# Block-sparse attention and a Gelu feed-forward on one core: sampled copies on VectorE alone, value loads tied to the feed-forward, values two rounds behind

## The chip, the core and the metric

One core of a Trainium2 chip runs the whole program. The metric is the device time of one execution in microseconds (us). The engines are named as the profile names them: PE (TensorE), DVE (VectorE), ACT (ScalarE), POOL (GpSimd), SP (SyncE). TensorE has two clock levels, 1.2 and 2.4 GHz; a granted clock of 1.00 is the upper one.

## The reference, cut to what matters

```python
# q, k, v: (4 batches, 8 heads, 768 rows, 64); blocks of 32 rows, 24 blocks; sampled_blocks: (24, 3)
scores = (q @ k.T) / 8
mask = |blk_i - blk_j| <= 1, or blk_i in (0, 23), or blk_j in (0, 23), or blk_j in sampled_blocks[blk_i]
attn = softmax(where(mask, scores, -1e9))
x    = (attn @ v), heads side by side          # (3072, 512)
out  = gelu_exact(x @ w_in) @ w_out            # 512 -> 2048 -> 512
```

## The kernel before

The work is cut into eight units: four batches times two halves of 12 blocks (384 rows). A unit's attention is followed by its first feed-forward product (FFN1: eight steps of eight 128x384 matmuls and one Gelu each, g holds the result), and its second one (FFN2: three output tiles of 16 matmuls) is cut into 48 pieces that fill the next unit's attention. The order on every engine is written out by hand; each engine runs its queue in order.

Attention goes by rounds. A first half has four dense rounds (blocks 0 and 23 see everything) and six sparse rounds of two query blocks; a second half has six sparse rounds. A round is: scores on PE (L218, 64x32 tiles of the array), a maximum on DVE (L252, L255), exponentials on ACT (L264), a 32x32 transpose on DVE (L281). Two rounds at a time then go through values on PE (L289, 128 small matmuls and as many weight loads), divided on DVE (L331), and outputs (L345: PE transposes, an ACT copy to xT). The scores buffers are two, the values buffer one. A sparse query block scores against three neighbours, blocks 0 and 23, and three sampled blocks: three products per head for each block.

The sampled blocks' keys and values are first copied into gb (L196): one copy for each of the 66 (block, sample) pairs of a batch, its source address in a register. DVE does 15 of them and POOL 51, into one gb for each half. For batch 0 keys and values are copied apart, since values come later. The registers are read once, at the start (L154).

The first unit has no feed-forward to hide behind (first_attention, L424): all its rounds run first, then DVE gathers its 15 value blocks, then come its values. When the next unit is a new batch, FFN1 is interleaved with prep (L168: PE transposes of k and q, copied into place by DVE for k and ACT for q), and the gather stands on DVE between the k part and the next unit's first maximum (L485 to L489).

All loads are issued by POOL, in its own order, behind its copies: for the next batch k, q and eight value loads (L474 to L480) are issued as the first half's FFN1 begins. The value loads have rows of 64 elements for each head.

Of the kernel before, what the change touches and what calls it, by code (L numbers as in the profile page):

```python
# [19 lines left out]
def kernel(  # L20
# [11 lines left out]
    P = 128  # L32
# [12 lines left out]
    BW = KC + 2 * V2  # L45
    PI = 8
# [4 lines left out]
    UB = NB // 2  # L51
    US = UB - 1
    NE = S // BL // 2
# [15 lines left out]
    gbs = [const.tile([P, US, NR, BW], BF16, name=f"gb{i}") for i in range(2)]  # L69
# [8 lines left out]
    g = const.tile([P, KOUT, UT], BF16, name="g")  # L78

    HALVES = (slice(0, 4), slice(4, 8))  # L80

# [24 lines left out]

    raw = const.tile([1, NB, NR, 2], I32, name="raw")
# [13 lines left out]

    def value_frame(i, engine):
        kv = kvs[i]
        engine.memset(kv[:, :, KC:BW], 0.0)
        for hh in range(4):
            c0 = KC + VW * (hh % 2) + D
            engine.memset(kv[32 * hh:32 * hh + 32, 0:NB, c0:c0 + V2 + 1:V2], 1.0)

# [5 lines left out]
    rf = const.tile([1, NB, NR], F32, name="rf")  # L134
    vf = const.tile([1, NB, NR], F32, name="vf")

    def value_list():
        inv = const.tile([1, NB, NR], F32, name="inv")
        tmp = const.tile([1, NB, NR], F32, name="tmp")
        nc.vector.tensor_copy(rf, raw[:, :, :, 0])  # L140
        nc.vector.tensor_tensor(tmp, rf, jrow, op=ALU.subtract)
        nc.vector.tensor_tensor(tmp, tmp, tmp, op=ALU.mult)
        nc.vector.tensor_scalar(inv, tmp, 1.0, None, op0=ALU.is_le)
        for c in (0.0, float(NB - 1)):
            nc.vector.tensor_scalar(tmp, rf, c, None, op0=ALU.is_equal)
            nc.vector.tensor_tensor(inv, inv, tmp, op=ALU.max)
        for a, c in ((1, 0), (2, 0), (2, 1)):
            nc.vector.tensor_tensor(tmp[:, :, 0], rf[:, :, a], rf[:, :, c], op=ALU.is_equal)
            nc.vector.tensor_tensor(inv[:, :, a], inv[:, :, a], tmp[:, :, 0], op=ALU.max)
        nc.vector.tensor_scalar(tmp, rf, -1.0, float(NB), op0=ALU.mult, op1=ALU.add)  # L150
        nc.vector.tensor_tensor(tmp, tmp, inv, op=ALU.mult)
        nc.vector.tensor_tensor(vf, rf, tmp, op=ALU.add)

    def block_numbers(js, engine):  # L154
        m = len(js)
        idx = const.tile([1, m, NR], I32, name=f"idx_{engine.name}_{js[0]}")
        nc.vector.tensor_copy(idx, vf[:, js[0]:js[0] + m, :])
        flat = idx.rearrange("o j r -> o (j r)")
        vals = []
        for c0 in range(0, m * NR, 22):  # L160
            c1 = min(c0 + 22, m * NR)
# [4 lines left out]
        return {(js[i // NR], i % NR): x for i, x in enumerate(vals)}  # L166

    def prep(b, which, pr, on_act):  # L168
        src = kn if which == "k" else qn
        pt = psT.tile([P, PI, PP], BF16, name="pt", tag="T")  # L170
        for i in range(PI):
            for h2 in range(2):
# [3 lines left out]
                                    identity[0:PP, 0:PP])  # L176
        if which == "k":
# [14 lines left out]
    def spare_key(b, engine):  # L192
        kT = keys(b)
        engine.tensor_copy(kT[:, NB, :], kT[:, 0, :])  # L194

    def gather(b, js, vals, engine, src=None, c0=0, c1=BW):  # L196
        src = kvs[b % 2][:, :, c0:c1] if src is None else src
        for j in js:
            gb = gbs[(j - 1) // US]
            for r in range(NR):  # L200
                engine.tensor_copy(gb[:, (j - 1) % US, r:r + 1, c0:c1],  # L201
                                   src[:, bass.ds(vals[j, r], 1), :])

    def gather_keys(js, vals, engine):
        gather(0, js, vals, engine, k0, 0, KC)

    def gather_values(js, vals, engine):
        gather(0, js, vals, engine, None, KC, BW)

    def rounds_of(hf):  # L210
        j0 = 1 + US * hf
        js = list(range(j0, j0 + US))
        dense = [("d", x, G) for x in (0, 1) for G in (0, 1)] if hf == 0 else []
        return dense + [("s", tuple(js[i:i + 2])) for i in range(0, US, 2)]
# [3 lines left out]
    def scores(b, rnd):  # L218
        qT, kT = qTs[b % 2], keys(b)
# [8 lines left out]
        if rnd[0] == "s":  # L228
            A4 = A.rearrange("p (g j c) -> p g j c", g=2, j=2)
            for i, j in enumerate(rnd[1]):  # L230
                gb = gbs[(j - 1) // US]
# [57 lines left out]
    def values(b, hf, grp):  # L289
        kv = kvs[b % 2]  # L290
# [13 lines left out]
        else:  # L304
            slots = [(rnd, i, j) for rnd in grp for i, j in enumerate(rnd[1])]
            for G in range(2):
                c0 = KC + V2 * G
                for c in range(8):
                    for s, (rnd, i, j) in enumerate(slots):
# [5 lines left out]
                        elif c < 5:  # L315
                            blk = (0, NB - 1)[c - 3]
                            blk = NB if abs(blk - j) <= 1 else blk
                            src = kv[:, blk, c0:c0 + V2]
                        else:
                            src = gbs[hf][:, (j - 1) % US, c - 5, c0:c0 + V2]  # L320
# [24 lines left out]
    def outputs(hf, grp):  # L345
# [7 lines left out]
        if grp[0][0] == "s":  # L353
            t0 = (grp[0][1][0] - UB * hf) * BL
            nc.scalar.copy(xTs[hf][:, :, t0:t0 + 32 * n], T[:, :, 0:32 * n])  # L355
        else:
            Tv = T[:, 0:2, :].rearrange("p h (g x q) -> p g h x q", g=2, x=2)
            for x, t0 in ((0, 0), (1, UT - BL)):
                nc.scalar.copy(
                    xTs[x][:, :, t0:t0 + BL].rearrange("p (g h) q -> p g h q", g=2), Tv[:, :, :, x, :])  # L360

    def ffn1_step(hf, m):
        hp = psA.tile([P, 2, 512], F32, name="hp", tag="A")
        for i in range(2):
            for ki in range(KIN):
                nc.tensor.matmul(hp[:, i, 0:UT], lhsT=w_in_sb[:, ki, (m + i) * P:(m + i + 1) * P],  # L366
                                 rhs=xTs[hf][:, ki, :], start=(ki == 0), stop=(ki == KIN - 1))
        nc.scalar.activation(g[:, m:m + 2, :], hp[:, :, 0:UT], AF.Gelu)  # L368

    def ffn2_pieces(b, hf):  # L370
        for t in range(UT // P):
# [8 lines left out]
            row = b * S + hf * UT + t * P  # L380
# [3 lines left out]
    def grouped(rounds, hf):  # L384

        ends = {}
        r0 = 0
        if hf == 0:
            ends[3] = tuple(rounds[0:4])
            r0 = 4  # L390
        for i in range(r0, len(rounds), 2):
            ends[min(i + 1, len(rounds) - 1)] = tuple(rounds[i:i + 2])
        return ends

    def attention(b, hf, filler):
        rounds = rounds_of(hf)
        n = len(rounds)
        ends = grouped(rounds, hf)
        late = 12
        per = -(-(KOUT * (UT // P) - late) // (n + 1))  # L400

        def fill(m):
            for _ in range(m):
                next(filler, None)
        for it in range(-1, n + 2):
            if it + 1 < n:
                scores(b, rounds[it + 1])
# [6 lines left out]
            fill(per // 2 if it <= n - 1 else late // 4)  # L414
            if it - 2 in ends:
                outputs(hf, ends[it - 2])
            if it - 1 in ends:
                values(b, hf, ends[it - 1])
                divided(ends[it - 1])
            fill(per - per // 2 if it <= n - 1 else late // 4)  # L420
        for _ in filler:
            pass

    def first_attention(fetch):  # L424

        rounds = rounds_of(0)
        n = len(rounds)
        for it in range(-1, n + 1):
            if it + 1 < n:
                scores(0, rounds[it + 1])  # L430
            if 0 <= it - 1 < n:
                turned(rounds[it - 1])
            if it + 1 < n:
                maxima(rounds[it + 1])
            if 0 <= it < n:
                exponentials(rounds[it])
        fetch()
        groups = list(grouped(rounds, 0).values())
        for i, grp in enumerate(groups):
            values(0, 0, grp)  # L440
            divided(grp)
            if i:
                outputs(0, groups[i - 1])
        outputs(0, groups[-1])

    units = [(b, hf) for b in range(B) for hf in range(2)]
    DVE, POOL = mybir.EngineType.DVE, mybir.EngineType.Pool
    J0, J1 = list(range(1, 1 + US)), list(range(1 + US, 1 + 2 * US))
    value_list()
    v_dve = block_numbers(J0[:5], DVE)  # L450
    v_pool0 = block_numbers(J0[5:], POOL)
    v_pool1 = block_numbers(J1, POOL)
    for pr in range(NPR):
        prep(0, "k", pr, False)
    for pr in range(NPR):
        prep(0, "q", pr, True)
    spare_key(0, nc.vector)
    gather_keys(J0[5:], v_pool0, nc.gpsimd)
    gather_keys(J0[:5], v_dve, nc.vector)
# [4 lines left out]
    gather_values(J0[5:], v_pool0, nc.gpsimd)  # L464
    gather_keys(J1, v_pool1, nc.gpsimd)
    gather_values(J1, v_pool1, nc.gpsimd)
    value_frame(1, nc.gpsimd)
    first_attention(lambda: gather_values(J0[:5], v_dve, nc.vector))

    for u, (b, hf) in enumerate(units):  # L470
        nxt = units[u + 1] if u + 1 < len(units) else None
        fresh = nxt is not None and nxt[1] == 0
        if hf == 0:
            if b + 1 < B:  # L474
# [51 lines left out]
```

## Time and profile before

| | us |
|---|---|
| median of 3 runs (range) | 410.44 (406.65 to 411.94) |
| profiled execution | 407.97 |
| its span | 405.8 |
| busy: PE, DVE, ACT, POOL | 280.7, 196.6, 202.8, 146.5 |

Busy shares say little here: no engine is busy more than 69% of the span, and each stage has its own limit. The profile is read by the chain of work that ended last, in order of time, and then by the stretch in which the chain waits.

### The profile page before, as it was taken

How to read it: one execution, taken by the hardware profiler on the slowest of the kernel's cores; microseconds unless marked ns; L12 is line 12 of the kernel's file. 1: busy time of each engine (PE TensorE's matmuls, PEld its weight loads, DVE VectorE, ACT ScalarE, POOL GpSimd, SP SyncE). 2: the span in 40 equal slices, each digit the busy share in tenths (PEclk: the TensorE clock that was granted, in tenths of full speed). 3: DMA queues.
4: the chain of work that ended last, by engine and by line, in shares of the span. 5: the costliest groups of instructions: out<-in, count | busy, mean ns of one | idle time of the engine just before them, and what ended most of it. 6: DMA issues, size and time to landing. Idle time of an engine off the chain costs nothing.

```text
span 405.8 us, 15457 instructions
## 1 busy us (share of the span) xinstructions
PE 280.7 (69%) x6889; PEld 161.2 (40%) x6952; DVE 196.6 (48%) x332; ACT 202.8 (50%) x344; POOL 146.5 (36%) x321
## 2 busy tenths in 40 slices
PE   0353304298789886697889764497789776977895
PEld 0222203144345353354444432254455343634542
DVE  6568993103636885106549771106538773065100
ACT  1057300057645775358456861258446764684531
POOL 8299997000002997100009992000007950000000
PEclk9999999999999999799999999599899999999999
DMA  8989709900010009920000049900000000000001
GB/s 125 105 100 206 118 0 162 75 0 2 31 53 4 1 31 153 117 20 29 31 27 2 28 69 162 61 0 31 29 28 2 29 29 31 0 29 29 29 26 52
DMA packets 39203, 20.90 MB, mean 52 GB/s; under 512 B 25825, under 2 KB 36066, under 8 KB 39138
## 3 DMA queue, kind: packets, MB, share of 16 engines
q0 software_dynamic: 35680, 13.63, 53.3%
q1 hardware_dynamic: 3458, 6.29, 4.2%
q8 instruction: 54, 0.88, 0.9%
q14 instruction: 11, 0.09, 0.1%
HBM read 27.26 MB, written 6.29 MB: 83 GB/s over the span
## 4 chain that ended last, share of the span: by engine, by line
PE 52%; DVE 18%; issue 15%; ACT 12%; DVEq 1%; ACTq 0%
PE hp L366 19%; PE op L374 13%; PE av L323 9%; ACT pp L264 7%; DVE gb L201 6%; PE sc L226 5%; PE pt L174 3%; DVE xh L340 3%; DVE nm L252 3%; ACT os L379 2%; ACT L264 2%; PE tx L350 2%; DVE nm L255 1%; PE av L299 1%; ACT xT L355 1%
## 5 line engine op out<-in xcount | busy, mean ns | idle before, releaser
L201 POOL COPY gb<-kv 128x388 bf16 (+1 forms) x204 | 88.6, 487 | 156.7 <-PE hp L366 101.5
L374 PE MATMUL op<-w_out_sb,g 128*128 128x512 bf16 x321 | 88.0, 384 | 19.6 <-ACT os L379 10.9
L264 ACT ACTIVATE pp<-sc,nm 128x256 bf16<-128x256 f32 (+1 forms) x192 | 92.6, 597 | 13.4 <-DVE nm L252 9.0
L366 PE MATMUL hp<-xT,w_in_sb 128*128 128x384 bf16 x512 | 95.7, 345 | 4.5 <-ACT xT L355 4.5
L252 DVE TENSOR_REDUCE nm<-sc 128x4 f32<-128x1024 f32 (+1 forms) x48 | 53.8, 1121 | 66.0 <-PE sc L226 65.3
L368 ACT ACTIVATE g<-hp 128x768 bf16<-128x768 f32 x64 | 51.9, 811 | 42.5 <-PE hp L366 42.5
L366 PEld LDWEIGHTS <-w_in_sb 128*128 128x128 bf16 x512 | 50.9, 103 | 41.3 <-issue 13.6
L323 PEld LDWEIGHTS <-pT 64*32 64x32 bf16 x2816 | 29.0, 98 | 65.6 <-issue 42.9
L323 PE MATMUL av<-kv,pT 64*32 64x130 bf16 x1760 | 29.0, 239 | 37.1 <-DVE xh L340 18.8
L374 PEld LDWEIGHTS <-g 128*128 128x128 bf16 x384 | 31.3, 98 | 38.3 <-issue 11.4
L226 PEld LDWEIGHTS <-qT 64*32 64x32 bf16 x2240 | 22.2, 93 | 50.4 <-issue 39.0
L336 DVE TENSOR_SCALAR den<-av 128x8 f32<-128x8 f32 (+2 forms) x28 | 4.8, 170 | 73.0 <-PE av L323 70.6
L201 DVE COPY gb<-kv 128x388 bf16 (+1 forms) x60 | 39.1, 838 | 1.1 <-DVE kv L194 1.0
L355 ACT COPY xT<-tx 128x512 bf16<-128x512 bf16 (+1 forms) x24 | 13.2, 552 | 49.0 <-PE tx L350 49.0
L379 ACT COPY os<-op 128x512 f32<-128x512 f32 x24 | 14.1, 588 | 42.5 <-PE op L374 27.5
L281 DVE STREAM_TRANSPOSE pT<-pp 128x512 f32<-128x512 f32 (+1 forms) x48 | 30.8, 653 | 5.7 <-ACT pp L264 5.5
L226 PE MATMUL sc<-kv,qT 64*32 64x96 bf16 (+3 forms) x1152 | 23.1, 211 | 10.5 <-ACT pp L264 9.7
L92 POOL DMA_DIRECT2D kv<-in_v_dram x32 | 22.7, 716 | 20.4 <-DMA qn<-in_q_dram 13.4
L323 PE MATMUL av<-gb,pT 64*32 64x130 bf16 x1056 | 21.5, 241 | 9.4 <-issue 9.4
L226 PE MATMUL sc<-gb,qT 64*32 64x96 bf16 x704 | 22.8, 214 | 3.6 <-issue 3.6
L188 ACT ACTIVATE qT<-pt 128x768 bf16<-128x768 bf16 x16 | 12.9, 806 | 20.3 <-PE pt L174 20.3
L183 DVE COPY kv<-pt 128x768 bf16<-128x768 bf16 x12 | 11.5, 958 | 17.0 <-PE pt L174 17.0
(50 smaller groups left out, 198.1 us busy)
## 6 DMA issues: line engine op xcount, KB each, us to landing
out_dram<-os SPq DMA_DIRECT2D x24, 256.0 KB, 2.1
kn<-in_k_dram POOLq DMA_DIRECT2D x8, 384.0 KB, 6.1
qn<-in_q_dram POOLq DMA_DIRECT2D x8, 384.0 KB, 9.1
kv<-in_v_dram POOLq DMA_DIRECT2D x32, 96.0 KB, 12.1
w_in_sb<-in_moe_w_in_dram POOLq DMA_DIRECT2D x4, 512.0 KB, 8.3
w_out_sb<-in_moe_w_out_dram POOLq DMA_DIRECT2D x2, 1024.0 KB, 18.1
raw<-in_sampled_blocks_dram SPq DMA_DIRECT2D x1, 0.6 KB
```

Of the source, the lines that this page charges most:

```text
L92: nc.gpsimd.dma_start(out=kvs[b % 2][32 * hh:32 * hh + 32, 0:NB, c0:c0 + D], in_=v[b, h].rearrange("(n p) d -> p n d", p=BL))
L201: engine.tensor_copy(gb[:, (j - 1) % US, r:r + 1, c0:c1], src[:, bass.ds(vals[j, r], 1), :])
L226: nc.tensor.matmul(o, lhsT=qT[rows, pr, BL * j:BL * j + BL], rhs=rhs[rows, :, BL * pr:BL * pr + BL], start=True, stop=True)
L252: nc.vector.tensor_reduce(out=nm[:, 0:2 * n].rearrange("p (g j) -> p g j", g=2), in_=A4[:, :, 0:n, :], op=ALU.max, axis=AX.X, negate=True)
L264: nc.scalar.activation(dst.rearrange("p (c k e) -> p c e k", e=2, k=BL), src.rearrange("p (c e k) -> p c e k", e=2, k=BL), AF.Exp, bias=bias)
L281: nc.vector.transpose(pt[:, 0:w].bitcast(F32), pp[:, 0:w].bitcast(F32))
L323: nc.tensor.matmul(av[32 * s:32 * s + 32, h, V2 * G:V2 * G + V2], lhsT=pv[rows, c // 2, :, c % 2], rhs=src[rows], start=(c == 0), stop=(c ...
L355: nc.scalar.copy(xTs[hf][:, :, t0:t0 + 32 * n], T[:, :, 0:32 * n])
L366: nc.tensor.matmul(hp[:, i, 0:UT], lhsT=w_in_sb[:, ki, (m + i) * P:(m + i + 1) * P], rhs=xTs[hf][:, ki, :], start=(ki == 0), stop=(ki == K ...
L368: nc.scalar.activation(g[:, m:m + 2, :], hp[:, :, 0:UT], AF.Gelu)
L374: nc.tensor.matmul(op, lhsT=g[:, m, t * P:(t + 1) * P], rhs=w_out_sb[:, m, :], start=(m == 0), stop=(m == KOUT - 1))
L379: nc.scalar.copy(os, op)
```

## The change

- POOL copies nothing any more. DVE does all sampled copies (33 for each unit), into one gb for both halves. The registers of the first half's blocks are kept; those of the second half are read anew by DVE in each batch, in two parts.
- A slot of gb has five blocks: keys of block 0, three sampled, keys of block 23 (two broadcast copies, gather_ends). A sparse block then has two score products per head, not three.
- In the first unit the eight transposed k and q tiles each have a PSUM space of their own, all placed by ACT.
- Value loads of batch b+1 or b+2 go four at a time behind the first Gelu of an FFN1 (hold_loads: a POOL copy of one element of g); k and q loads go behind its last Gelu. In the head, four value loads of batch 1 are issued after the weights.
- In a round the order on PE becomes scores, values (two rounds behind), outputs (three behind), FFN2 pieces. Groups of rounds follow the tiles of 128 rows.

```diff
-    gbs = [const.tile([P, US, NR, BW], BF16, name=f"gb{i}") for i in range(2)]
+    gb = const.tile([P, US * GW + BW - KC], BF16, name="gb")
+    def hold_loads(m):
+        nc.gpsimd.tensor_copy(mark, g[0:1, m, 0:1])
...
+    def gather_ends(b, n):
+        ends = gb[:, 0:GW * n].rearrange("p (j c) -> p j c", c=GW)
+        for c0, blk in ((0, 0), (4 * BW, NB - 1)):
+            nc.vector.tensor_copy(ends[:, :, c0:c0 + KC],
+                                  keys(b)[:, blk:blk + 1, :].to_broadcast([P, n, KC]))
+    def gather(b, js, *spans):
+        for k0_, k1 in ((0, len(js)),) if js[0] in known else ((0, 6), (6, len(js))):
+            part = js[k0_:k1]
+            at = known if js[0] in known else block_numbers(part, DVE)
+            for i, j in enumerate(part, k0_):
+                for r in range(NR):
+                    for c0, c1 in spans:
+                        src = keys(b) if c1 == KC else kvs[b % 2][:, :, c0:c1]
+                        nc.vector.tensor_copy(slot(i)[:, 1 + r:2 + r, c0:c1],
+                                              src[:, bass.ds(at[j][r], 1), :])
...
                 for c0, c1, rhs in ((0, 96, kT[:, j - 1:j + 2, :]),
-                                    (96, 160, kT[:, 0:NB:NB - 1, :]),
-                                    (160, 256, gb[:, (j - 1) % US, :, :])):
+                                    (96, 256, slot(unit.js.index(j)))):
...  (attention)
+        tail = (4, 9)
+        share = max(0.0, pieces - sum(tail)) / (n + 3)
+        for it in range(-1, n):
+            if it + 1 < n:
+                scores(unit, rounds[it + 1])
+            if it - 2 in ends:
+                values(unit, ends[it - 2])
+            if it >= 1:
+                turned(rounds[it - 1])
+            if it + 1 < n:
+                maxima(rounds[it + 1])
+            if it - 2 in ends:
+                divided(ends[it - 2])
+            if it >= 0:
+                exponentials(rounds[it])
+            if it - 3 in ends:
+                outputs(unit, ends[it - 3])
+            fill(share * (2 if it < 1 else 1))
...  (head)
-    gather_keys(J0[5:], v_pool0, nc.gpsimd)
-    gather_keys(J0[:5], v_dve, nc.vector)
+    for i, (which, pr) in enumerate([(w, pr) for w in "kq" for pr in range(NPR)]):
+        turn_heads(which, pr, spaces[i])
+        place_heads(0, which, pr, spaces[i], True)
+    spare_key(0)
+    gather(0, units[0].js, (0, KC))
+    gather_ends(0, len(units[0].js))
...
+    value_frame(1, nc.gpsimd, 5)
+    for h in range(4):
+        load_v(1, h)
...  (loop over units)
+        if nxt is not None and not fresh:
+            if b == 0:
+                gather(0, nxt.js, (0, KC), (KC, BW))
+            else:
+                gather(b, nxt.js, (0, BW))
+            gather_ends(b, len(nxt.js))
         for s in range(KOUT // 2):
+            ffn1_step(n, 2 * s)
+            if s == 0:
+                if not fresh and b + 1 < B:
+                    hold_loads(0)
+                    for h in range(4, H):
+                        load_v(b + 1, h)
+                if fresh and b + 2 < B:
+                    hold_loads(0)
+                    for h in range(4):
+                        load_v(b + 2, h)
+            if s == 7 and not fresh and b + 1 < B:
+                hold_loads(14)
                 for hs in HALVES:
                     load_kq(kn, k, b + 1, hs)
```

## Rows read from the trace of the kernel before

**Rows 1.** The page: the span, and the queue that brings instructions.

```profile
span 405.8 us, 15457 instructions
...
q8 instruction: 54, 0.88, 0.9%
```

**Rows 2.** The chain that ended last, in order of time: start us, length us, what.

```profile
67.20 2.34 issue
...
73.32 6.53 issue
...
82.66 13.12 PE hp L366 x64
...
136.37 0.87 DVE nm L255
...
168.19 13.10 PE hp L366 x64
...
221.41 0.87 DVE nm L255
...
251.02 6.12 issue
...
260.41 13.00 PE hp L366 x64
...
298.12 1.46 PE hp L366 x8
...
314.43 0.87 DVE nm L255
...
329.10 1.52 issue
...
379.11 10.56 PE hp L366 x64
```

**Rows 3.** Timeline of the head: start us, us, engine, line, work [idle before, releaser].

```profile
12.72 0.71 POOL L92 DMA_DIRECT2D kv<-in_v_dram  x1 [1.24 <-DMA qn<-in_q_dram]
...
18.58 0.85 PE L174 MATMUL pt<-identity,qn 96*64 96x96 bf16 x16 [1.05 <-DVE qT L183]
...
19.47 0.81 ACT L188 ACTIVATE qT<-pt 128x768 bf16<-128x768 bf16 x1 [17.44 <-PE pt L174]
...
25.49 1.91 DVE L255 TENSOR_REDUCE nm<-sc 128x1 f32<-128x768 f32 x2 [3.44 <-PE sc L226]
...
42.19 11.52 POOL L201 COPY gb<-kv 128x260 bf16 x33
...
44.32 17.56 DVE L201 COPY gb<-kv 128x260 bf16 x15
...
62.63 0.74 PE L323 MATMUL av<-kv,pT 64*32 64x130 bf16 x40 [17.13 <-DVE xh L340]
```

**Rows 4.** DVE's copies beside POOL's and alone (timelines); the register reads (by line).

```profile
129.30 7.08 DVE L201 COPY gb<-kv 128x388 bf16 x15 [0.39 <-DVE kv L194]
...
60.81 0.70 DVE L201 COPY gb<-kv 128x260 bf16 x4
...
18.80 0.45 DVE L201 COPY gb<-qT 128x128 bf16 x3
...
L162 DVEq TENSOR_LOAD <-idx_DVE x1: 1778/1778/1778, 9.9 to 9.9; - x1
```

**Rows 5.** Stretches: length, busy PE, PEld, DVE, ACT, POOL; granted clock, DMA share, GB/s.

```profile
238.00:249.00 11.00, 6.23 (x216) 3.15 (x218) 5.14 (x10) 5.29 (x12) 7.23 (x11) 0.84 1.05 171
249.00:259.00 10.00, 2.97 (x105) 1.85 (x104) 1.52 (x5) 0.92 (x2) 0.73 (x2) 0.81 3.72 79
...
343.94:354.50 10.56, 10.56 (x77) 6.23 (x83) 0.00 (x0) 6.93 (x8) 0.00 (x0) 1.00 0.04 15
```

**Rows 6.** Timeline of one sparse round in a second half.

```profile
275.24 0.45 PEld L226 LDWEIGHTS <-qT 64*32 64x32 bf16 x48 [0.42 <-issue]
...
275.88 1.23 DVE L252 TENSOR_REDUCE nm<-sc 128x4 f32<-128x1024 f32 x1 [0.68 <-PE sc L226]
```

More of the change, by code (lines that the diff above doesn't have):

```diff
@@ L204, in gather_keys, with prep @@
[L204 to L214, printed above, removed]
+    def prep(b, which, pr, on_act):
+        pt = psT.tile([P, PI, PP], BF16, name="pt", tag="T")
+        turn_heads(which, pr, pt)
+        place_heads(b, which, pr, pt, on_act)
@@ new lines, with __init__ @@
+    class Unit:
+        def __init__(self, b, quads, dense):
+            self.b, self.quads, self.dense = b, quads, dense
+            self.groups = [[j for j in range(4 * t, 4 * t + 4) if 0 < j < NB - 1] for t in quads]
+            self.js = [j for grp in self.groups for j in grp]
+            self.rounds = [("d", x, G) for x in (0, 1) for G in (0, 1)] if dense else []
+            self.ends = {3: tuple(self.rounds)} if dense else {}
+            for grp in self.groups:
+                r = [("s", tuple(grp[i:i + 2])) for i in range(0, len(grp), 2)]
+                self.rounds += r
+                self.ends[len(self.rounds) - 1] = tuple(r)
@@ L216, with scores @@
+    units = [Unit(b, quads, dense) for b in range(B) for quads, dense in (((0, 1, 2), True), ((3, 4, 5), False))]
+    column = {}
+    for n, unit in enumerate(units):
+        for t, quad in enumerate(unit.quads):
+            for i in range(4):
+                column[unit.b, 4 * quad + i] = (xTs[n % 2], P * t + BL * i)
     st = {}
-    def scores(b, rnd):
-        qT, kT = qTs[b % 2], keys(b)
+    def scores(unit, rnd):
+        qT, kT = qTs[unit.b % 2], keys(unit.b)
         A = psA.tile([P, 1024], F32, name="sc", tag="A")
@@ L287, in turned, with values @@
                 pp[:, 0:S].bitcast(F32).rearrange("p (c k) -> p c k", k=BL))
-    def values(b, hf, grp):
-        kv = kvs[b % 2]
+    def values(unit, grp):
+        kv = kvs[unit.b % 2]
         av = psV.tile([P, 2, 512], F32, name="av", tag="V")
@@ L365, in ffn1_step, with ffn2_pieces @@
             for ki in range(KIN):
[L366 to L371, printed above, removed]
+                nc.tensor.matmul(hp[:, i, 0:T], lhsT=w_in_sb[:, ki, (m + i) * P:(m + i + 1) * P],
+                                 rhs=xTs[n % 2][:, ki, 0:T], start=(ki == 0), stop=(ki == KIN - 1))
+        nc.scalar.activation(g[:, m:m + 2, 0:T], hp[:, :, 0:T], AF.Gelu)
+    def ffn2_pieces(n):
+        for t, quad in enumerate(units[n].quads):
             op = psO.tile([P, D_MODEL], F32, name="op")
@@ L379, in ffn2_pieces, with attention @@
             nc.scalar.copy(os, op)
-            row = b * S + hf * UT + t * P
+            row = units[n].b * S + quad * P
             nc.sync.dma_start(out=out[row:row + P, :], in_=os)
             yield
[L384 to L396, printed above, removed]
+    def attention(unit, filler, pieces):
+        rounds, ends = unit.rounds, unit.ends
@@ new lines, in attention, with first_attention @@
+        if n - 2 in ends:
+            values(unit, ends[n - 2])
+        turned(rounds[n - 1])
+        if n - 2 in ends:
+            divided(ends[n - 2])
+        if n - 3 in ends:
+            outputs(unit, ends[n - 3])
+        fill(tail[0])
+        values(unit, ends[n - 1])
+        divided(ends[n - 1])
+        if n - 2 in ends:
+            outputs(unit, ends[n - 2])
+        fill(tail[1])
+        outputs(unit, ends[n - 1])
+        for _ in filler:
+            pass
+    def first_attention(unit):
+        rounds = unit.rounds
+        n = len(rounds)
+        for it in range(-1, n + 1):
+            if it + 1 < n:
+                scores(unit, rounds[it + 1])
@@ L413, in attention @@
                 exponentials(rounds[it])
[L414 to L438, printed above, removed]
+        gather(0, unit.js, (KC, BW))
@@ L439, in first_attention @@
+        groups = list(unit.ends.values())
         for i, grp in enumerate(groups):
-            values(0, 0, grp)
+            values(unit, grp)
             divided(grp)
             if i:
[L443 to L448, printed above, removed]
-    value_list()
-    v_dve = block_numbers(J0[:5], DVE)
@@ L451 @@
[L451 to L457, printed above, removed]
-    gather_keys(J0[5:], v_pool0, nc.gpsimd)
-    gather_keys(J0[:5], v_dve, nc.vector)
+                outputs(unit, groups[i - 1])
+        outputs(unit, groups[-1])
+    DVE = mybir.EngineType.DVE
+    value_list()
+    known = block_numbers(units[0].js, DVE)
+    spaces = [psA.tile([P, 2, 1024], BF16, name="pk", tag="A") for _ in range(2)]
@@ L494 @@
         else:
-            attention(*nxt, filler)
+            attention(nxt, filler, KOUT * len(unit.quads))
 _INS = ['q', 'k', 'v', 'sampled_blocks', 'moe_w_in', 'moe_w_out']
```

135 lines of the change are left out of this document (63 added, 72 removed).

## Prediction

> **What bounds the kernel now.** I read the span first: 405.8 us, and no more can be had from the busy shares, since no engine is full [rows 1]. Then I read the chain that ended last in order of time, to cut the run into stages [rows 2]. FFN1 of the first unit starts at 82.66, so the head, which makes one eighth of the attention, takes a fifth of the run. After it the run repeats by batch: a FFN1 of 10.6 or 13 us; attention of a second half (343.94 + 10.56 to 379.11 and 260.41 + 13.00 to 298.12, 24.6 and 24.7 us, two of four); FFN1 with prep (298.12 to 314.43, 16.3 us); attention of a first half with its dense rounds. The last one should be equal for all batches and is not: 136.37 to 168.19, 221.41 to 260.41, 314.43 to 343.94, so 31.8, 39.0 and 29.5 us. The reader should ask what the long ones wait for.
>
> Two things. One is "issue", a wait of PE for nothing that the profile shows: 2.34, 6.53 and 6.12 us at a time, always in the many small matmuls of values [rows 2]. The instruction queue brought 0.88 MB in 54 packets, so one packet for each 15457/54 = 286 instructions, and a values group alone has 256 [rows 1]. The long waits stand where value loads fill the DMA engines: from 249 to 259 the DMA share is 3.72 at only 79 GB/s, and PE is busy 2.97 us of 10; with k and q landing (238 to 249) the share is 1.05 at 171 GB/s and PE does better [rows 5]. I read this as instructions that arrive late behind thousands of small packets. The batch with no load has waits too, but short (1.52 at 329.10 and a second like it) [rows 2]. The other is the sampled copies in the head: PE sits 17.13 us before its first sparse values, waiting for DVE, whose 15 copies of 260 columns take 17.56 us beside POOL's 33 [rows 3]. Four such copies take 0.70 us when POOL's are over, and three of 128 columns 0.45 [rows 4]. So alone they cost about 0.175 and 0.15 each; beside POOL 15 copies of 388 columns took 7.08, 0.47 each.
>
> **The head.** Before, k and q tiles went through one PSUM space, PE and copy in turn; now the eight go on without waiting. The second half of q is in SBUF at about 12.7 (POOL's queue waited for it); two PE turns of 0.85 and a placement of 0.81 then end at 15.2 [rows 3]. DVE is the later one. Its list ends at about 9.9 with a register read of 1.78 behind it [rows 4]; with some seven small operations fewer it ends near 8.3. Two reads (22 numbers at most in one) make 11.9, 33 key copies at 0.15 make 16.9, and two end copies, 1408 columns each, are not in the trace: between one copy of 128 columns (0.15) and eleven of them (1.65), I take 0.7 each. That is 18.3, and the first maximum at 18.5, where it was 25.49 [rows 3]: 7.0 gained. The rounds from there to the value copies took 44.32 - 25.49 = 18.8 and keep that, bound by the same exponentials: 37.3. Then 33 value copies at 0.175 = 5.8, done at 43.1, not 61.9. So PE's sparse values start at about 43.8 rather than 62.63. From there to FFN1 were 20.0 us, of which 8.87 were the waits of 2.34 and 6.53 [rows 2]. The weights and half the next batch's values are still landing then, so I put one wait of 2.3 back: 13.5. FFN1 starts at 57.3: **-25.3**. With no wait it is 55; with a long one of 6.5 it is 61.5.
>
> **FFN1.** The two that follow the long waits take 13.1 and 13.0 us [rows 2]; one that follows none takes 10.56 at a granted clock of 1.00, while the stretch before the slow one was granted 0.81 [rows 5]. If the waits go, both should take 10.56: **-5.0**. The first unit's stays at 13.1, as PE is mostly idle before it in the head.
>
> **Attention of the first halves.** No load is issued in it any more. The third, without its two short waits, is 29.5 - 3.0 = 26.5. I leave 0.8 of waiting in, because scores and values now stand side by side, a longer burst than before: 27.3 three times = 81.9 instead of 100.3: **-18.4**.
>
> **Attention of the second halves.** Here k and q of the next batch now land (three of four). From 238 to 249 such loads cost PE some waiting but no long stop [rows 5]; I take 1.5 each, bounds 0 and 4: +4.5. On the other side, a change of the tile shape costs up to 0.42 before the first weight load, and one value group in two rounds needs one change less; 16 of a round's 48 score products go, at 0.45/48 = 0.009 each, 0.15 a round [rows 6]. At most that is 0.57 for each of six rounds, 3.4 a unit. But DVE's maximum alone is 1.23 a round, and DVE, ACT and PE take turns, so most of PE's gain becomes idle time: I take 1.0 a unit, -4.0, and nothing in the first halves (bounds 0 and -3.4). Values a round later should cost nothing, as the next round's scores cover it; uncovered it is one group's values and division at the end of a unit, which stands there already. Sum **+0.5**.
>
> **The gathers.** 33 copies of 388 columns alone are not in the trace. Bounds are 0.175 (260 columns alone) and 0.47 (388 beside POOL) [rows 4]; I take 0.19, nearer to the copies without POOL. With prep: 33 x 0.19 + 1.4 = 7.7 us, where DVE spent 7.08 on 15; the next maximum waits behind it, but also for q's placement: nothing. In a second half: two reads of 1.78, 6.3 and 1.4, 11.3 us, hidden by FFN1 (10.56 and about 1 us that DVE is free before it): nothing, but there is no slack either, and every us more is paid at once by the next unit's scores. In batch 0 keys and values are copied apart: 33 x 0.325 + 3.6 + 1.4 = 15.7 against 14.1: **+1.6**. What POOL still does, a copy of one element that waits for a Gelu with four DMAs of about 0.7 behind it [rows 3], is late for nobody: these loads are needed one or two units later. The Gelu of the next unit would wait for that copy, a whole unit after it.
>
> **Sum.** -25.3 - 5.0 - 18.4 + 0.5 + 1.6 = -46.6. The profiled execution took 407.97 (2.2 outside its span), so 361.4; the median of the runs, 410.44, is 1.006 of it, so **363 us**.
>
> **A rule against this change.** POOL's DMA issues stand at 0.71 in the head, before any copy runs beside them [rows 3]; the trace has no value load issued beside a long row of DVE copies. The Trainium skill (SBUF — State Buffer, the box on the "DVE blocks DMA" trap in the section on two separate sides) says that while VectorE runs a copy in a two-port mode, GpSimd cannot write the descriptors of its DMAs. By it the value loads, now issued just when DVE gathers, would come late; no run here shows it, and the price follows from rows as the second rival.
>
> **Rivals.** *First: instructions come late without loads as well.* For it: 1.52 at 329.10 with nothing landing; and 64 products and weights of scores now stand right before 256 of values. Against it: most groups of that batch had no such wait, and a sparse round has a quarter fewer PE instructions in its scores. At 1.5 for each of 24 groups, less the 7 us that the sum holds already, +29: about 391; at half the groups 374.
>
> *Second: value loads slip out of FFN1 into attention*, since DVE's copies hold up their issue. They are half as large, so a wait of about 4.4 (between 2.34 and 6.53) in six attentions, 26 more, and two FFN1 slow again, 5: about 394. Against it: an FFN1 has some 7 us left after the issue.
>
> *Third, the other side: DVE's copies are as slow alone as beside POOL.* At 0.47 instead of 0.19, 33 copies are 9.2 us more in each of seven gathers, none of it hidden, and 33 x (0.3 + 0.1) = 13 in the head: 78 more, 441, slower than before. It decides at the pitch where the 47 us are eaten, about 0.36. Against it: 0.175 for 260 columns is already faster than 0.47 in proportion.
>
> *Fourth: the waits have nothing to do with loads.* Then the head keeps its 8.9 and the first halves theirs, 18.4 and 5.0 come back: about 394. Against it stands the quiet batch.
>
> *Fifth, better:* no wait is left anywhere, the head ends at 55 and the PE saving counts in all units: about 349.
>
> **How the numbers follow.** Forecast 0.62, first rival 0.14 (mostly the half case), second 0.08, third 0.04, fourth 0.02, fifth 0.10. The range 346 to 388 takes in the fifth, the half case of the first and a head with a long wait; the whole first, the second, third and fourth are left out, under 0.2. The likeliest case alone, with the bounds of its terms: 352 to 374. A measurement here can tell about 2% from no change: under 402 is faster. All but the third case lie there: faster 0.94, within 0.02, slower 0.04.
>
> **What the profile would show.** Right: FFN1 of the first unit starts near 57; DVE's copies come 0.15 to 0.2 us apart; DMA share is high inside FFN1 and low in attention of first halves; these take 27 to 28 us each, all alike; FFN1 takes 10.6 from the second batch on; the waits called "issue" are under 2 us. Wrong: copies at 0.3 or more apart; the first scores after a plain FFN1 waiting for DVE's gather; long waits of PE in values with loads in flight, or without.

## The result, and the profile after

The changed kernel takes 368.4 us in the median (364.7 to 372.5), the kernel before 409.7; the ratio is 0.895, with an interval of 0.885 to 0.905. Forecast were 363 us. The profiled execution of the changed kernel, 370.89 us with a span of 368.9, is one of its slow runs, which the ratio leaves out. Its head is 6 us longer than in some of the runs below, and why is itself a result.

The page of the changed kernel, its first part and the DMA slices (mean busy share of the 16 DMA engines, 40 slices):

```profile
span 368.9 us, 14062 instructions
...
PE 270.0 (73%) x6209; PEld 153.9 (42%) x6248; DVE 215.9 (59%) x590; ACT 204.3 (55%) x348; POOL 48.3 (13%) x78
...
DMA  8999900957092001956190001990000000000001
...
kv<-in_v_dram POOLq DMA_DIRECT2D x32, 96.0 KB, 5.7
```

1395 instructions are gone, nearly all from PE, and POOL is busy for a third of its former time. Value loads land 5.7 us after their issue. The stages, in us, cut at the start of the first and of the last FFN1 matmul of each unit (the chain of [rows 2] counts to the end of the last one, so its FFN1 are 0.16 longer):

| stage | before | after | change | forecast |
|---|---|---|---|---|
| head, to the first FFN1 | 82.66 | 63.55 | -19.1 | -25.3 |
| FFN1 without prep, five | 12.96, 12.94, 12.83, 10.40, 10.40 | 12.29, 11.50, 11.50, 10.40, 10.40 | -3.4 | -5.0 |
| FFN1 with prep, three | 14.37 each | 14.37 each | 0 | 0 |
| first halves, three | 33.66, 40.94, 31.45 | 30.23, 28.99, 31.35 | -15.5 | -18.4 |
| second halves, four | 24.54, 23.97, 24.88, 24.77 | 25.77, 23.47, 26.13, 23.90 | +1.1 | +2.1 |
| last FFN2 | 16.3 | 16.3 | 0 | 0 |
| span | 405.8 | 368.9 | -36.9 | -46.6 |

(The forecast's 1.6 for batch 0's gather stands with the second halves, whose start it delays.) So the two large terms have the right place and sign, and the head is 6 us short. This is the head on DVE and on POOL (timelines: start us, us, engine, line, work):

```profile
16.29 2.63 DVE L227 COPY gb<-qT 128x128 bf16 x20
19.24 8.01 DVE L227 COPY gb<-qT 128x128 bf16 x13 [0.32 <-issue]
26.96 1.27 DVE L215 COPY gb<-qT 128x1408 bf16<-128x1408 bf16 x2
28.16 0.93 DVE L287 TENSOR_REDUCE nm<-sc 128x1 f32<-128x768 f32 x1
...
20.28 0.87 POOL L107 DMA_DIRECT2D w_out_sb<-in_moe_w_out_dram  x1 [0.45 <-DMA kv<-in_v_dram]
21.14 5.69 POOL L119 MEMSET kv<- 128x1300 bf16 x5
```

Twenty key copies go at 0.13 each; then, from 21.14, POOL writes the frame of the second value buffer (its zeros, and the ones beside the values) and the last copies stand until 26.8, when it is done. I call this the lock. It is what rows 3 showed for POOL's copies, now with a memset. The trace before had that too: right behind its 33 copies POOL writes a frame, and DVE's first two value copies, begun at 44.32 and 53.36, end only at 59.25 and 59.32.

```profile
53.66 5.50 POOL L124 MEMSET kv<- 128x6500 bf16 x1
```

The copies beside FFN1 with prep, where POOL is quiet, against the first line of [rows 4]:

```profile
110.75 5.70 DVE L227 COPY gb<-kv 128x388 bf16 x33 [0.39 <-DMA kv<-in_v_dram]
116.37 1.01 DVE L215 COPY gb<-kv 128x1408 bf16<-128x1408 bf16 x2
117.30 0.94 DVE L287 TENSOR_REDUCE nm<-sc 128x1 f32<-128x768 f32 x1
```

0.17 each (forecast 0.19), and 0.5 for an end copy (forecast 0.7). PE's waits under issue on the chain, the longer ones:

```profile
88.82 1.40 issue
...
132.79 1.65 issue
...
167.61 1.42 issue
...
248.51 2.54 issue
...
300.62 2.14 issue
...
328.80 2.16 issue
```

Against 6.53 and 6.12 in [rows 2] none is over 2.6; but the last two stand in batch 3, with no load in flight.

### The profile page after: what moved, and what is told of

Read it like the earlier page. It is cut to its first block, busy times and chain, and to the rows that moved or that the text cites. A ratio compares the mean times of both kernels' runs of the same rounds, so it can differ in the third digit from the quotient of the medians.

```text
span 368.9 us, 14062 instructions
## 1 busy us (share of the span) xinstructions
PE 270.0 (73%) x6209; PEld 153.9 (42%) x6248; DVE 215.9 (59%) x590; ACT 204.3 (55%) x348; POOL 48.3 (13%) x78
## 4 chain that ended last, share of the span: by engine, by line
PE 43%; DVE 20%; ACT 13%; issue 10%; DMA 9%; POOL 3%; DVEq 1%; ACTq 0%; POOLq 0%
PE hp L400 14%; PE op L408 14%; DMA kv<-in_v_dram 9%; PE av L355 8%; DVE gb L227 6%; ACT pp L296 5%; DVE nm L284 4%; ACT os L413 3%; ACT L296 2%; PE sc L260 2%; DVE nm L287 2%; DVE xh L372 2%; POOL kv L119 2%; PE tx L382 1%; DVE ptd L317 1%
## 5 line engine op out<-in xcount | busy, mean ns | idle before, releaser
L296 ACT ACTIVATE pp<-sc,nm 128x256 bf16<-128x256 f32 (+1 forms) x192 | 92.0, 590 | 31.5 <-DVE nm L287 16.3
L408 PE MATMUL op<-w_out_sb,g 128*128 128x512 bf16 x345 | 91.1, 390 | 15.9 <-ACT os L413 11.7
L400 PE MATMUL hp<-xT,w_in_sb 128*128 128x384 bf16 x512 | 90.3, 331 | 8.9 <-ACT xT L387 7.0
L400 PEld LDWEIGHTS <-w_in_sb 128*128 128x128 bf16 x512 | 49.0, 99 | 42.2 <-issue 12.3
L227 DVE COPY gb<-kv 128x388 bf16 (+1 forms) x264 | 48.1, 252 | 13.2 <-issue 12.1
L408 PEld LDWEIGHTS <-g 128*128 128x128 bf16 x384 | 32.7, 99 | 48.1 <-issue 18.8
L355 PE MATMUL av<-kv,pT 64*32 64x130 bf16 x1760 | 33.7, 236 | 16.8 <-issue 8.4
L260 PEld LDWEIGHTS <-qT 64*32 64x32 bf16 x1536 | 15.6, 95 | 60.2 <-issue 48.9
L260 PE MATMUL sc<-kv,qT 64*32 64x96 bf16 (+2 forms) x624 | 18.1, 226 | 11.2 <-ACT pp L296 11.2
L113 POOL COPY mark<-g 1x1 bf16<-1x1 bf16 x8 | 1.5, 189 | 181.9 <-ACT g L402 181.9
L260 PE MATMUL sc<-qT,qT 64*32 64x96 bf16 (+2 forms) x208 | 8.6, 288 | 21.6 <-ACT pp L296 21.3
L260 PE MATMUL sc<-gb,qT 64*32 64x160 bf16 x704 | 18.5, 245 | 1.9 <-DVE gb L215 1.2
```

Source lines behind the costliest of these rows:

```text
L227: nc.vector.tensor_copy(slot(i)[:, 1 + r:2 + r, c0:c1], src[:, bass.ds(at[j][r], 1), :])
L260: nc.tensor.matmul(o, lhsT=qT[rows, pr, BL * j:BL * j + BL], rhs=rhs[rows, :, BL * pr:BL * pr + BL], start=True, stop=True)
L296: nc.scalar.activation(dst.rearrange("p (c k e) -> p c e k", e=2, k=BL), src.rearrange("p (c e k) -> p c e k", e=2, k=BL), AF.Exp, bias=bias)
L355: nc.tensor.matmul(av[32 * s:32 * s + 32, h, V2 * G:V2 * G + V2], lhsT=pv[rows, c // 2, :, c % 2], rhs=src[rows], start=(c == 0), stop=(c ...
L400: nc.tensor.matmul(hp[:, i, 0:T], lhsT=w_in_sb[:, ki, (m + i) * P:(m + i + 1) * P], rhs=xTs[n % 2][:, ki, 0:T], start=(ki == 0), stop=(ki ...
L408: nc.tensor.matmul(op, lhsT=g[:, m, t * P:(t + 1) * P], rhs=w_out_sb[:, m, :], start=(m == 0), stop=(m == KOUT - 1))
```

## The experiments

Each kernel is the changed one with one edit, if nothing else is said, and stage lengths are cut as in the table.

**Loads at once.**

```diff
-  (value loads behind the first Gelu, k and q behind the last)
+        if not fresh and b + 1 < B:      # ahead of the first half's FFN1, nothing held
+            k, q and eight value loads of batch b + 1
```

> The changed kernel, but each batch's k, q and eight value loads stand together ahead of the first half's FFN1, as in the kernel before, and nothing holds them back. Theory (PE's long waits in values come from value loads in flight): attention of the first halves of batches 1 and 2 grows from 30.2 and 29.0 us to between 33 and 41, with waits of PE of 2 to 6 us under issue; attention of batch 3, with no load beside it, stays near 31; the whole is 10 to 18 us longer than the changed kernel's 364 to 369, so about 380, ratio to the kernel before about 0.93. Rival (the waits came from POOL's copies or from something else that is gone): no stage moves by more than 2 us and the time stays at 364 to 370.

373.8 us, ratio 0.919 (0.907 to 0.931). First halves of batches 1 and 2 take 34.61 and 33.78, 4.4 and 4.8 more; batch 3 keeps 31.38. The chain of this kernel has one long wait in each of the two:

```profile
130.79 4.59 issue
...
210.83 4.37 issue
```

and the stretch around the first (as [rows 5]) shows a DMA share of 1.96 at only 76 GB/s and PE busy 3.41 us of 8:

```profile
128.00:136.00 8.00, 3.41 (x160) 2.39 (x139) 2.86 (x7) 2.23 (x6) 0.00 (x0) 0.98 1.96 76
```

So value loads in flight do cost PE long waits: 9.2 us in the two units. But in the profile nearly all of it is given back: second halves beside no load are 6.6 shorter in all (23.40, 21.75, 23.65), and FFN1 of units 2 and 4, which hold no loads, 2.2 (10.40 each). What remains is 2.6 in the head, where all loads of batch 1 now land and PE waits 2.19 in values at 57.00. The profiled spans differ by 2.9 (371.8 against 368.9), the medians by 5.4. So where the change puts the loads, they cost other stages almost as much as they cost here. The kernel before lost more (40.94); its loads, behind POOL's copies, fell on the values at the end of the unit, here they fall on its dense rounds. Whether that is the reason was not tried alone.

**The frame on VectorE.**

```diff
-    value_frame(1, nc.gpsimd, 5)      # after the weight loads
+    value_frame(1, nc.vector)         # after value_list()
```

> The changed kernel, but the frame of the second value buffer (the memsets) is written by VectorE right after its list, not by GpSimd after the weight loads. Theory (in the head three key copies of VectorE stood 6.3 to 6.5 us behind GpSimd's memsets of 5.69 us): the first maximum, at 28.16 us in the changed kernel, comes at 21 to 23, the first FFN1 starts at 57 to 58 instead of 63.55, and the whole is 5 to 7 us shorter, about 361. Rival (the copies wait for something else, such as instructions that arrive late, and the memsets only stand beside it): the first maximum stays at 27 to 29, or later by the 2.8 us that the memset takes on VectorE.

366.6 us, ratio 0.900 (0.891 to 0.908). The copies no longer stop (33 in 4.67 us), but the register reads begin 3.4 us later, behind the memsets: first maximum 25.44, first FFN1 60.70. It lies between theory and rival: the lock is gone, and half of it is paid for.

**Holding on xT instead of g.**

```diff
-        nc.gpsimd.tensor_copy(mark, g[0:1, m, 0:1])
+        nc.gpsimd.tensor_copy(mark, xTs[n % 2][0:1, KIN - 1, UT - BL - 1:UT - BL])   # value loads only
```

> The changed kernel, but the copy of one element that holds the value loads back reads the last column of the FFN1's input (xT), not the first Gelu's output g; the k and q loads still wait for the last Gelu. Theory (because GpSimd reads g, the next unit's first Gelu has one wait more, and ScalarE then loads its table only after the first product: FFN1 of units 2 and 4 took 11.5 us with a gap of 0.94 us before the third step, where units 6 and 7, behind no such read, took 10.4): FFN1 of units 2 and 4 falls to 10.4, 2.2 us in all. Rival (the gap is VectorE's gather or the loads beside that FFN1, which stay): both stay at 11.5. The whole moves by less than 1% either way.

363.7 us, ratio 0.896 (0.888 to 0.903). FFN1 of units 2 and 4 is 10.40 each. ACT at the start of unit 2's FFN1, first the changed kernel, then this one:

```profile
147.75 1.28 ACT L402 ACT_TABLE_LOAD   x1 [1.59 <-PE hp L400]
149.05 1.51 ACT L402 ACTIVATE g<-hp 128x768 bf16<-128x768 f32 x2
```

```profile
142.21 1.28 ACT L405 ACT_TABLE_LOAD   x1
143.74 0.81 ACT L405 ACTIVATE g<-hp 128x768 bf16<-128x768 f32 x1 [0.25 <-PE hp L403]
```

With POOL reading g, the table load waits for PE's product; without it the load runs while PE computes. The theory holds. The whole is 4.7 less, more than the 2.2 at stake, since the run also gave what was not asked. In its head the weight loads held POOL 1.7 us longer, and the memsets met no copy:

```profile
19.24 1.71 DVE L230 COPY gb<-qT 128x128 bf16 x13 [0.34 <-issue]
20.87 1.44 DVE L218 COPY gb<-qT 128x1408 bf16<-128x1408 bf16 x2
22.23 1.80 DVE L290 TENSOR_REDUCE nm<-sc 128x1 f32<-128x768 f32 x2
...
22.82 5.69 POOL L122 MEMSET kv<- 128x1300 bf16 x5
```

First FFN1 at 57.67, where the forecast had 57.3. The head is a race. Of the eight profiles with the memsets on POOL behind the weight loads and nothing to order them, three won it: DVE's end copies are done at 22.0 to 22.3, the memsets start at 22.5 to 22.8, the first maximum at 21.9 to 22.2. Five lost it: the memsets start at 21.1 to 22.1, the first maximum at 28.2 to 28.6. The runs of the changed kernel (364.7 to 368.7, and 370.9 and 372.5) fit this, but only one of them has a trace, so it is not shown for the others.

**The order before.**

```diff
-  scores, values (two behind), outputs, pieces
+  scores, half the pieces, outputs, values (one behind), the other half
```

> The changed kernel, but attention in the order of the kernel before: values one round behind, outputs two, FFN2 pieces in two parts between them, twelve kept for the end. Theory (the order is worth at most 1 us a unit, since VectorE, ScalarE and TensorE take turns; the first half without loads took 31.45 us before and 31.35 after): attention with no loads beside it (batch 3, both halves: 31.4 and 23.9 us) moves by at most 1.5 us each, and the whole is 0 to 6 us longer. Rival (the order carries much of the gain): first halves 2 us or more longer each, second halves 2 us, 12 to 16 us in all, about 380.

366.6 us, ratio 0.891 (0.879 to 0.903), not to be told from the changed kernel. First halves are shorter (28.17, 27.82, 28.45: 6.1 in all), second halves longer (29.29, 26.38, 25.58, 23.73: 5.7 in all). In three other profiles in which these stages are as in the changed kernel (the frame on VectorE, holding on xT, the frame early) first halves sum to 87.9 to 89.9 and second halves to 100.2 to 101.5, where the changed kernel has 90.6 and 99.3; so the effects are 3.5 to 6.1 and 3.5 to 5.7. The new order pays in second halves only, and there in batches 0 and 1.

**POOL shares the copies.**

```diff
+  eng, at = (nc.vector, known) if i < 5 else (nc.gpsimd, known_pool)    # head values, gathers with prep
```

> The changed kernel, but GpSimd takes 18 of the 33 copies beside VectorE's 15 again, in the head's value copies and in the three gathers with prep. Theory (the two engines shut each other out, so sharing is slower than VectorE alone, 0.17 us a copy): with prep VectorE's 15 copies take about 7 us (0.48 each) and the next unit's first maximum comes 1 to 1.5 us later after FFN1; in the head the value copies take 8 to 11 us instead of 4.56; 6 to 11 us in all. Rival (two engines copy more than one, the gain of the change lay elsewhere): the gathers take no longer and the time stays within 2 us.

375.8 us, ratio 0.924 (0.917 to 0.931): 7.3 more. In the gathers the theory holds: DVE's 15 copies take 7.1 us, the first maximum behind FFN1 comes 1.7 to 2.0 us later, and first halves take 33.29, 29.98 and 33.55. In the head it does not: POOL does its share while DVE still works on rounds, and from the first maximum to FFN1 it is 33.8 us, not 35.4.

**No later loads** (k, q and v of batch 0 serve for all batches).

> The changed kernel without any load of k, q and v after batch 0 (all batches use what is in the buffers) and without the copies that hold loads back. What remains of waits is not from loads. Theory (k and q beside the second halves cost 1 to 2 us each, the hold copy 1.1 in FFN1 of units 2 and 4, and first halves have no load any more): second halves of batches 0 to 2 fall from 25.8, 23.5 and 26.1 to 22 to 24, FFN1 of units 2 and 4 to 10.4, first halves stay at 29 to 31; 5 to 8 us less in all, and PE's waits of about 2 us at the end of batch 3 stay. Rival (no wait is left that loads cause): nothing moves but the 2.2 us of FFN1.

359.6 us, ratio 0.883 (0.877 to 0.890). Second halves of batches 0 to 2 take 23.44, 21.75 and 24.71: k and q beside them cost 2.3, 1.7 and 1.4. FFN1 of units 2 and 4 is 10.40, and first halves lose 0.6 to 2.2, the 2.2 in batch 3, where neither kernel has a load in flight; so much can lie between two profiles. The waits of batch 3 stay on the chain, with no load since the weights:

```profile
290.89 2.17 issue
...
318.46 1.75 issue
```

**Three products.**

```diff
-                                    (96, 256, slot(unit.js.index(j)))):
+                                    (96, 160, kT[:, 0:NB:NB - 1, :]),
+                                    (160, 256, slot(unit.js.index(j))[:, 1:4, :])):
```

> The changed kernel, but a sparse block scores again in three products per head (neighbours; blocks 0 and 23; sampled blocks), 16 more on PE for each round; the copies of the end blocks' keys stay. Theory (PE waits for VectorE and ScalarE in most rounds, so the products saved are mostly idle time): 0 to 4 us longer in all. Rival (PE's instructions set the pace, 0.15 us a round and fewer packets of instructions): 46 rounds make 7 us or more.

380.1 us, ratio 0.936 (0.928 to 0.944): 11.7 more in the median, 6.3 in the profiled spans (375.2 against 368.9), whose heads are alike (63.37 and 63.55). How much of the 11.7 is the race in the head is not known; 6.3 is near the rival's 7 and beyond the theory's 4. In the profile the second halves of batches 0 and 1 carry most of it (29.19 and 26.93, 3.4 and 3.5 more), both beside k and q; that of batch 2, beside them too, does not (25.82). The wait of 1.42 at 167.61 in the changed kernel is here

```profile
171.52 3.63 issue
```

So the products were not idle time of PE. That the instructions themselves come late can be read from the traces. In the changed kernel the instruction queue brought 49 packets for PE's 12466 recorded instructions, one for about 254 (54 packets here, as in the kernel before). In the trace of the last experiment below, PE has five waits of over 1 us under issue. They stand behind its first 2241, 4289, 8897, 10945 and 11713 instructions. Each of these is 193 more than a multiple of 256, and the multiples, 8, 16, 34, 42 and 45, are the numbers of packets begun by then. So PE stops where the next packet is needed, and goes on 2.3 to 2.7 us after that packet begins on the queue.

In fourteen traces there are 90 such waits of over 0.9 us; in eight of the traces all 45 have the same remainder of 193, in the six others it falls along the trace (to 135 at the lowest), as it would with records missing. No two packets begin less than 3.3 us apart, while PE takes 1.2 to 2.0 for the 256 instructions of a values group. Beside value loads a packet also begins late: 1.6 us into the wait of 4.59 in the run with the loads at once and 2.7 into the one of 6.12 in the kernel before, but 0.1 ahead of the one of 2.14 at 300.62 in the changed kernel. From 298 to 304 the changed kernel moves hardly anything else (DMA, all queues, then the one that brings instructions):

```profile
DMA packets 11, 0.05 MB, mean 8 GB/s; under 512 B 3, under 2 KB 3, under 8 KB 9
...
q8 instruction: 2, 0.03, 2.4%
```

**Pieces between scores and values.**

```diff
             if it - 2 in ends:
+                fill(2)
+                due[0] -= 2
                 values(unit, ends[it - 2])
```

> The changed kernel, but two FFN2 pieces stand between a round's scores and its values (two fewer after it), so that 64 and 256 small PE instructions no longer follow each other. Theory (waits of about 2.1 us in values with no load in flight come from instructions that arrive late in a long burst): these waits of batch 3, 2.14 and 2.16, fall under 1 us and its halves shorten by 1 to 2 us each, though two tile shape changes more cost up to 0.5 for each values group. Rival (256 instructions of values alone are enough for the wait): waits of 1.5 us or more remain and the halves get longer by the shape changes, 0.5 to 1.5 us each.

370.4 us (367.0 to 374.6). The halves of batch 3 take 31.64 and 24.65, 0.3 and 0.8 more, no more than other profiles differ by. On the waits the rival holds: one stays in values that now follow a piece (chain):

```profile
323.29 0.38 PE op L408
323.67 1.15 PE av L355 x121
324.81 1.67 issue
326.48 0.29 PE av L355 x7
```

It comes after 121 of 128 matmuls, where the next packet is due, the 45th, as for the wait at 328.80 in the changed kernel: moving two pieces does not change how many instructions PE takes in.

**The frame early.**

```diff
     for h in range(H):
+        if h == 2:
+            value_frame(1, nc.gpsimd, 5)
         load_v(0, h)
...
-  22 block numbers in a read
+  18
```

> The changed kernel, but GpSimd writes the second value buffer's frame after the second value load, at about 6.5 to 14 us, when VectorE reads registers; and block numbers are read 18 at a time, not 22. Theory (key copies of VectorE and memsets of GpSimd meet in the head when the memsets begin before the copies are over at about 21 us: first maximum at 28.2 and first FFN1 at 63.4 when they meet, 22.0 and 57 when they do not, in the kernels run so far): they never meet, the first maximum comes at 19 to 22.5, the first FFN1 at 54 to 58, and the whole is at 357 to 363 without the runs near 370. Rival (value loads and weights, 7.6 us later on GpSimd's queue, become the limit, or the reads of 18 are no shorter): first FFN1 at 60 or later.

371.9 us, ratio 0.919 (0.913 to 0.926); first maximum 28.82, first FFN1 63.84. My place for it was wrong, and it shows the lock once more. The memsets now meet the first operation of DVE's list, a cast of 72 numbers on one partition (0.26 us in the changed kernel):

```profile
5.54 6.69 DVE L151 CAST rf<-raw 1x72 f32<-1x72 int32 x1
...
6.50 5.69 POOL L119 MEMSET kv<- 128x1300 bf16 x5
12.24 1.32 POOL L122 MEMSET kv<- 32x48 bf16 x4
```

Reads of 18 and 15 numbers took 4.4 and 3.4 us, in sum what 22 and 11 had taken.

**Loads moved** (with the early frame).

```diff
+  k, q of batch b + 1 behind xT of the first half (batch 0: behind its last Gelu)
+  eight value loads of batch b + 2 behind xT of the FFN1 with prep (batch 1: of the first FFN1)
```

> As the run with the early frame; loads are held by the last column of xT, not by g; k and q of the next batch go into the first half's FFN1 (batch 0: behind its last Gelu, as in the changed kernel), eight value loads go into FFN1 with prep two batches ahead (batch 1: into the first unit's FFN1). Theory (k and q beside the second halves cost 1.4 to 2.3 us each, seen without any load; FFN1 has room): second halves of batches 1 and 2 fall to 21.5 to 24.5, FFN1 of units 2 and 4 to 10.4; 5 to 7 us less than the run with the early frame. Rival (eight value loads do not fit into the 14.4 us of FFN1 with prep, or k and q not into 10.4): waits of 2 to 5 us at the start of first or second halves, and no gain.

365.0 us, ratio 0.901 (0.895 to 0.906), 6.9 less than with the early frame alone, though its head is as slow (63.93). FFN1 of units 2 and 4 is 10.40; second halves of batches 1 and 2 take 23.02 and 24.19 (23.46 and 26.24 there), first halves 29.81, 27.90, 30.05 (30.26, 29.10, 30.57).

**Mixed order** (with the loads moved; first halves in the order before).

> As the run with the loads moved, and first halves go in the order of the kernel before (values one round behind), second halves stay two behind. Theory (with the order before, first halves took 28.2, 27.8 and 28.5 instead of 30.2, 29.0 and 31.4, second halves up to 3.5 longer): first halves at 27 to 28.5, 3 to 7 us less than the run with the loads moved, about 348 to 354 in all. Rival (the shorter first halves came from that run's luck with late instructions): no difference beyond 2 us.

360.9 us, ratio 0.890 (0.882 to 0.898), 4.1 less. First halves take 27.77, 28.11 and 29.23, 2.7 less in all; one of them is a little above what was expected, and that of batch 1 is no shorter than before (27.90). Second halves, which the edit leaves alone, are 2.5 shorter in all. The 348 to 354 expected took the early frame for a gain, which it was not.

**The frame behind the gather** (with the mixed order; the frame after the weight loads again).

```diff
+    nc.gpsimd.tensor_copy(mark, gb[0:1, 4 * BW:4 * BW + 1])      # waits for DVE's end copies
     value_frame(1, nc.gpsimd, 5)
```

> As the run with the mixed order, but the frame's memsets stand after the weight loads again, as in the changed kernel, with a copy of one element ahead of them that waits for VectorE's end copies; block numbers are read 22 at a time again. Theory (a memset of GpSimd costs the head about 6 us whenever a copying VectorE instruction meets it, be it a key copy or the first cast of the list, and nothing when it meets maxima from PSUM): the first maximum comes at 21.5 to 22.5 and the first FFN1 at 56.5 to 58 in every run, so 5 to 7 us less than with the early frame, about 352 to 356, and the runs lie closer together. Rival (the memset then costs VectorE's transposes as much): first FFN1 at 61 or later, no gain.

356.6 us (354.4 to 358.2), ratio 0.874 (0.869 to 0.879): better than both kernels. The memset begins when the maxima do, and disturbs none of them:

```profile
22.31 1.80 DVE L290 TENSOR_REDUCE nm<-sc 128x1 f32<-128x768 f32 x2
22.45 0.18 POOL L532 COPY mark<-gb 1x1 bf16<-1x1 bf16 x1 [0.92 <-DVE gb L218]
22.57 5.66 POOL L122 MEMSET kv<- 128x1300 bf16 x5
23.28 2.07 ACT L299 ACTIVATE pp<-sc,nm 128x768 bf16<-128x768 f32 x2 [7.35 <-DVE nm L290]
```

First FFN1 at 57.53, 6.1 earlier than in the run with the mixed order. The whole gained 4.3 and ends just above the 352 to 356 expected: the second half of batch 0, beside k and q, took 28.05 instead of 26.38, with a wait of 3.94 at 81.10.

## Why the prediction was right, and where it was not

*The head.* Right in mechanism. The list ended at 8.14 (8.3), the rounds took 18.8 (18.8), the 33 value copies 4.56 (5.8), and the values had no long wait (11.2 us to FFN1, 13.5 put). Two steps failed. The step "two reads make 11.9" was mis-sized: I took 1.78 for each from DVE's one row; POOL's three reads in that trace (22, 22 and 7 numbers) took 1.74, 1.78 and 2.50. The reads by line:

```profile
L170 DVEq TENSOR_LOAD <-vf x10: 1570/2952/5193, 8.2 to 307.4; - x10
```

The first, of 22 numbers, took 5.19 and the second, of 11, 2.52: first maximum 3.7 late. And the step "33 key copies at 0.15" took the copies as alone, since POOL copied nothing any more. I overlooked POOL's memsets, though the diff shows them moved to just behind the weight loads: 6 us where they meet. Where they do not meet, three profiles have the first FFN1 at 57.1 to 57.7, by chance so near to 57.3, since the late reads and the shorter values cancel.

*FFN1.* The waits went and with them the slow FFN1s, but the step "late for nobody", on the copy that holds loads, failed: POOL's read of g put a wait ahead of the next unit's table load, 1.1 us in units 2 and 4. The first unit's FFN1, left at its old length, gave 0.7 of the 3.4. I had checked who waits for POOL, not what the extra wait does to the order on ACT.

*First halves.* The cause was right: the waits are instructions that come late, later still beside value loads, and the run with the loads at once loses 9.2 of the 15.5 again (what the rest is was not split). 15.5 came of 18.4. The step "values a round later should cost nothing" failed: the new order costs them 3.5 to 6.1 us in all.

*Second halves.* k and q cost 2.3, 1.7 and 1.4 (1.5 put). But the step "most of PE's gain becomes idle time" was mis-sized: with three products second halves take 6.0 us more in the profile, and the order is worth 3.5 to 5.7 there, where I had 4.0 for both. The errors hid each other: +1.1 came where +2.1 was put.

*Gathers.* Right: 0.17 a copy; in batch 0 PE waited 1.17 for the end copies (1.6 put).

*Rivals.* The first is half true: waits of about 2.1 do come without loads, but in few groups. The second did not come: the four value loads from 150.43 on were issued in 0.74 each beside DVE's copies and landed in 4.9 to 6.0. So the rule of the Trainium skill on VectorE's copies and GpSimd's descriptors (SBUF — State Buffer, SBUF: two separate sides) had no price here that these rows show. The third, fourth and fifth are out.

*The sum.* The profiled span is 9.7 us beyond the forecast: 6.2 in the head, 2.9 in first halves and 1.6 in FFN1, less 1.0 in second halves. (361.4 times 1.006 is 363.6, not 363.)

## What to carry to other kernels

When work is taken off an engine because it holds up another, list everything that engine still does, memsets and one-element copies too, and order it behind the other engine's copies: here one wait was worth 6 us in the head, and six runs with it lie within 3.8 us, where those of the changed kernel lie within 7.8. A read added only for its timing makes its tile's next writer wait, so hang it on a tile whose writer has nothing to set up. Two changes that look like one gain (order, placement of loads) should be tried by stage, since one stage can pay for another. Where an engine runs hundreds of small instructions, count them against the packets of the instruction queue.

## What the hardware showed that I had not expected

- A DVE copy that meets POOL's memsets waits for the whole row, not for one: the longest took 6.47 us in the changed kernel, beside five memsets of 5.69 in all. It began 0.7 us before them, during a DMA issue of POOL. Such an issue holds DVE's copies too: those from 16.80, 18.06 and 19.24 end at 17.30, 18.55 and 19.82, and the issues beside them at 17.30, 18.56 and 19.83. The memset followed the last issue without a gap. A cast of 72 numbers on one partition was shut out as well (6.69 instead of 0.26); maxima read from PSUM and transposes were not (0.90 and 0.58 beside the memsets of the last experiment).
- Reading block numbers into DVE's registers took 0.22 to 0.25 us a number in the head (5.19 for 22, 2.52 for 11, 4.4 for 18, 3.4 for 15) and in the second read of later gathers (3.4 to 3.7 for 15), but 1.57 for the first 18 of every later gather of the changed kernel. What makes the first one cheap was not settled.
- PE stops for about 2 us now and then with no load in flight, always where a new packet of 256 instructions is due; packets begin at least 3.3 us apart. Neither two pieces before a burst nor the absence of loads took that away.
